# Softmax weights of two batches turned by DMA instead of TensorE, in a fused attention, gated MLP and mixture-of-experts kernel

## The chip, the cores and the metric

The kernel runs on one core of a Trainium2 chip. The metric is the device time of one execution in microseconds (us). One core has TensorE (PE in the profile; weight loads are PEld), VectorE (DVE), ScalarE (ACT), GpSimd (POOL), SyncE (SP, which only issues DMAs here), 16 DMA engines, the on-chip memory SBUF and the matmul result memory PSUM.

## The reference

Three layers in float32, each feeding the next:

```
# attention: 4 batches, 8 heads, 576 positions, head size 64; each query sees at most 32 keys of a band
scores = scale * q @ k.T ; scores = where(mask, scores, -1e9)
attn = exp(scores - max) / (sum + 1e-9) ; x = attn @ v          # x: 2304 tokens x 512
# gated layer
x = ((x @ w_a) * (x @ w_b)) @ w_out                             # 512 -> 1536 -> 512
# routed layer: each token goes to the one of 8 experts with the best cosine score
out[tok] = gate[tok] * (relu(x[tok] @ w1[e]) @ w2[e])
```

## The kernel before

Matrix products keep float32 accuracy by splitting each operand into a high part (`hi`, a rounded copy made by ScalarE) and a low part (`lo`, the remainder, a subtraction on VectorE), and adding three products (`mm3`, lines 768 to 770).

The outer loop runs over batches b = 0 to 3. For each, `f_step(b, f)` is called for f = 0 to 11, one for each 128 columns of the hidden size 1536. A step multiplies the batch's tokens by one slice of w_a and w_b: 24 matmuls of 128x512 for b = 1 and b = 2 (`mm(0, 0)` gives a, `mm(1, 0)` gives b), then `a_copy` (ScalarE, line 813), the product `g` (VectorE, line 819) and, one step later, the high and low parts of g (`g_lows`: ScalarE line 822, POOL line 823). The same step also splits the next step's weight slice, which SyncE has fetched (`ab_load`, line 723): `hi` on ScalarE (line 726), `lo` on VectorE (line 727). After the 12 steps `x1_run` multiplies by w_out.

Woven into the steps of batch b is the attention of batch b + 1, in units of 64 queries, two units to a pair (`AttnPair`; five pairs, the last with one unit). This text says even and odd step for even and odd f; a pair takes an even step, the odd step behind it and the next even one. Before the change, for b = 1 and 2:

- even step: TensorE makes the pair's scores after the first six matmuls of the step (line 584); VectorE adds the mask and takes the maximum for each unit (lines 602, 606); POOL scales the maxima (`least`, line 609); ScalarE takes the exponentials of unit 0 (line 616); VectorE and POOL divide by the sums (`norm`, lines 623 to 625).
- odd step: exponentials and `norm` of unit 1 at its start; in its middle TensorE turns unit 0's weights with four transposes (`trans`, line 633) and ScalarE copies them out of PSUM (line 635).
- next even step: unit 1 is turned at the start, and after six matmuls TensorE makes the products with v (`av`, line 644), directly ahead of the next pair's scores. ScalarE and VectorE then split the result into x0h and x0l (lines 659, 661).

Also in these steps, VectorE computes 32 router dot products ("logits", line 265) for the tokens of the batch before. `Router.steps` takes a list of counts that it cycles through, two entries to a step. SyncE is one queue in program order; in the loop of batch 1 it also issues eight `prefill` writes of 786 KB to memory (line 181). In every engine instructions run in program order, so a waiting one holds all behind it. The program order is written by hand.

Of the kernel before, what the change touches and what calls it, by code (L numbers as in the profile page):

```python
# [87 lines left out]
def fused_kernel(ctx: ExitStack, tc: tile.TileContext, qk, v, wab, wout, w1, w2, emb, tau, cst, msk, out, dbg=None):  # L88
# [380 lines left out]
    class Attn:  # L469
# [3 lines left out]
        def scores(self):  # L473
            b, j = self.b, self.j
            t, jj = qkt[b, j // 3], j % 3
            both = ps.two("odd" if j % 2 else "pair", "sc")[:, :, :192].rearrange("p o (h c) -> p o h c", h=2)
            self.sc = [both[:, odd] for odd in range(2)]
            mt = MASK_OF.get(j, 1)
            m0 = 0 if j == 0 else 1
            if mt == m0:  # L480
                mask = mask_bf[:, mt:mt + 1, :].to_broadcast([128, 2, 96])
            else:
                mask = mask_bf[:, m0:mt + 1:mt - m0, :]
            for sc in self.sc:
                nc.tensor.matmul(out=sc, lhsT=id_bf, rhs=mask, start=True, stop=False)
            for h in range(2):
                for odd in range(2):
                    for p in range(2):
                        pr = 2 * h + odd
                        q = p ^ odd  # L490
                        nc.tensor.matmul(
                            out=self.sc[odd][64 * q:64 * q + 64, h, :],
                            lhsT=t[64 * p:64 * p + 64, pr, 64 * jj:64 * jj + 64],
                            rhs=t[64 * p:64 * p + 64, pr, 192 + 64 * jj:192 + 64 * jj + 96],
                            start=False, stop=h == 1,
                        )
            self.s = at.tile([128, 4, 96], F32, tag="s", name="s", bufs=4)
            mx = at.tile([128, 4], F32, tag="amx", name="amx")
            nc.vector.tensor_reduce(out=mx.rearrange("p (h o) -> p o h", o=2), in_=both, axis=AX.X, op=ALU.max, negate=True)
            self.src = [self.sc[pr % 2][:, pr // 2, :] for pr in range(4)]  # L500
            self.least = at.tile([128, 4], F32, tag="least", name="least")
            nc.gpsimd.tensor_scalar(out=self.least, in0=mx, scalar1=0.125, scalar2=None, op0=ALU.mult)

        def exp(self):
            self.sm = at.tile([128, 4], F32, tag="asm", name="asm")
# [50 lines left out]
    class AttnPair:  # L556
# [33 lines left out]

        def least_of(self):
            n = self.n
            self.s = [at.tile([128, 4, 96], F32, tag="s", name="s", bufs=4) for _ in range(n)]
# [26 lines left out]
        def norm(self, i):  # L620
            if i < self.n:
# [2 lines left out]
                nc.vector.reciprocal(out=sm, in_=sm)  # L624
                nc.gpsimd.tensor_tensor(out=s, in0=s, in1=sm.unsqueeze(2).to_broadcast([128, 4, 96]), op=ALU.mult)

        def trans(self, i):
            if i < self.n:
                if i == 0:
                    self.aT = []  # L630
                tp = ps.tile([96, 4, 128], F32, tag="tp", name="atp")
                for pr in range(4):
                    nc.tensor.transpose(tp[:, pr, :], self.s[i][:, pr, :], ident)
                self.aT.append(at.tile([96, 4, 128], F32, tag="aT", name="aT"))
                nc.scalar.activation(out=self.aT[i], in_=tp, func=AF.Copy)
# [12 lines left out]
                            start=True, stop=True,  # L648
                        )

        def oevac(self):
            hi, lo = x0[self.b]
# [5 lines left out]
            for kk, i, ln, dst in parts:  # L658
                nc.scalar.activation(out=dst(hi), in_=self.o[:, kk, i:i + ln], func=AF.Copy)
            for kk, i, ln, dst in parts:  # L660
                nc.vector.tensor_tensor(out=dst(lo), in0=self.o[:, kk, i:i + ln], in1=dst(hi.bitcast(F32)), op=ALU.subtract)

    def pairs_of(b):
        return [AttnPair(b, list(range(j, min(j + 2, NJ))), b == 1) for j in range(0, NJ, 2)]

    ab_raw, ab_hl = {}, {}
# [124 lines left out]
    def g_lows():  # L791
        while g_low:
            g_low.pop(0)()

    def f_step(b, f, pairs, extra, extra2):
# [6 lines left out]
        prv = pairs[p - 1] if not odd and 0 <= p - 1 < len(pairs) else None  # L802

        def mm(c, hf, ks=range(4)):
            for k in ks:
# [3 lines left out]
        kept = {}  # L809

        def a_copy(hf):
            kept[hf] = ap.tile([128, CH], F32, tag="a", name="a")[:, :CHUNKS[b][hf]]
            nc.scalar.activation(out=kept[hf], in_=acc[0, hf], func=AF.Copy)

        def g_evac(hf):
# [10 lines left out]

        if f - lag in (3, 6, 9):
            load_qk()
        if f - lag in (5, 8, 11):
            load_v()  # L830
        if f < NF - 2:
            ab_load(n + 2)
        if b == 0 and n < 10:
            conv_load(n + 4)
        if n == NF - 1:
# [23 lines left out]
            ab_split(n + 1)  # L859
        else:  # L860
            wo_split(b * NF)
        if len(CHUNKS[b]) == 1:
            mm(0, 0, (0, 1))
            if not odd:
                if prv is not None:
                    prv.av()
                if cur is not None:
                    cur.open()
                    cur.scores()
                    cur.least_of()  # L870
                if prv is not None:
                    prv.oevac()
            g_lows()
            mm(0, 0, (2, 3))
            a_copy(0)
            if cur is not None and not odd:
                cur.exp(0)
            for x in extra:
                x()
            mm(1, 0, (0, 1))  # L880
            if cur is not None and odd:
                cur.trans(0)
            for x in extra2:
                x()
            mm(1, 0, (2, 3))
            if cur is not None and not odd:
                cur.norm(0)
            g_evac(0)
            del ab_hl[n]
            return  # L890
        mm(0, 0)
        a_copy(0)
        if not odd:
# [390 lines left out]
    with tc.manual_schedule():  # L1284
# [61 lines left out]
        for b in range(B):  # L1346
# [5 lines left out]
                pairs = []  # L1352
            steps = iter(())
            if router is not None:
                steps = router.steps((2, 2) if last else (1, 0, 2, 2))
            for f in range(NF):
                extra = []
                extra2 = []
# [25 lines left out]
            if not last:  # L1384
# [13 lines left out]
                if b == B - 2:  # L1398
# [7 lines left out]
                    for q in range(2):  # L1406
                        nc.gpsimd.tensor_copy(out=x0_end[q][:, :, :2 * CARRY], in_=x0_in[b][q][:, :, CH:])
                        nc.gpsimd.tensor_copy(out=x0_end[q][:, :, 2 * CARRY:], in_=x0[b + 1][q][:, :, END0:])
                x1_run(b, hook)
                for _ in steps:  # L1410
                    pass
# [248 lines left out]
```

## Time and profile before

| | |
|---|---|
| time, median of 3 runs | 769.56 us (769.0 to 771.37) |
| time of the profiled execution | 770.28 us |
| its span, first to last instruction | 768.4 us, so 1.9 us lie around it |
| busy TensorE, VectorE, ScalarE, POOL | 98%, 67%, 56%, 30% of the span |
| steps of batch 1, of batch 2 | 79.80 us, 79.64 us (12 steps each) |
| TensorE's granted clock | 1.00 over the span |

The busy share of TensorE says that nearly all of the span has a matmul in it. What a microsecond of another engine's work is worth depends on whether TensorE waits for it in that stretch.

### The profile page before, as it was taken

The page shows a single profiled execution, that of the slowest core. Times are in us where ns is not written, and L with a number is a line of the kernel's source. Part 1 is how long each engine was busy: PE and PEld are TensorE (multiplying, and loading weights), DVE is VectorE, ACT ScalarE, POOL GpSimd, SP SyncE. Part 2 cuts the span into 40 slices and gives each one's busy share as a digit, 9 for nine tenths or more (in the row PEclk, how much of TensorE's full clock was granted, in tenths as well). Part 3 has the DMA queues.
Part 4 walks back from the last instruction along what each step waited for, and adds up shares of the span by engine and source line. Part 5 has one row for each costly group of instructions (what it writes and reads, how often), then busy time and mean ns, then how long its engine had stood idle before and what let it go on. Part 6 is the DMA issues. An engine that isn't in the chain of part 4 may idle for free.

```text
span 768.4 us, 14431 instructions
## 1 busy us (share of the span) xinstructions
PE 755.8 (98%) x5411; PEld 673.4 (88%) x5411; DVE 514.2 (67%) x1067; ACT 429.2 (56%) x950; POOL 229.9 (30%) x261
## 2 busy tenths in 40 slices
PE   8899999999999999999999999999999999999996
PEld 4799998878878888888899999899888999999995
DVE  4788888758887468986267763354666565765672
ACT  5767764356653267662334442375585666767571
POOL 3644444023434224344223524224110001101111
PEclk9999999999999999999999999999999999999999
DMA  9977878577942424222421122835666747757821
GB/s 345 360 235 260 279 278 293 189 276 249 340 159 93 166 65 186 84 83 81 167 71 68 55 83 88 243 110 194 165 226 200 197 135 212 187 169 220 229 90 37
DMA packets 61055, 137.65 MB, mean 179 GB/s; under 512 B 27410, under 2 KB 27666, under 8 KB 58544
## 3 DMA queue, kind: packets, MB, share of 16 engines
q1 hardware_dynamic: 57888, 127.09, 50.7%
q0 software_dynamic: 3088, 9.55, 3.3%
q8 instruction: 44, 0.72, 0.4%
q14 instruction: 35, 0.29, 0.1%
HBM read 106.04 MB, written 25.87 MB: 172 GB/s over the span
## 4 chain that ended last, share of the span: by engine, by line
PE 85%; issue 5%; DMA 4%; DVE 3%; ACT 2%; POOL 1%; POOLq 0%; ACTq 0%; DVEq 0%
PE mm L768 13%; PE mm L770 13%; PE mm L769 12%; PE xr L768 4%; PE xr L769 4%; PE xr L770 4%; DMA out_dram<-yo,ixi 4%; PE hp L770 3%; PE hp L769 3%; PE hp L768 3%; PE xm L770 2%; PE xm L768 2%; PE xm L769 2%; PE ytp L770 2%; PE ytp L768 2%
## 5 line engine op out<-in xcount | busy, mean ns | idle before, releaser
L768 PE MATMUL mm<-x0h,ab 128*128 128x288 f32 (+2 forms) x480 | 171.2, 357 | 0.0
L770 PE MATMUL mm<-x0h,ab 128*128 128x288 f32 (+2 forms) x480 | 166.9, 348 | 0.2 <-DVE ab L727 0.2
L769 PE MATMUL mm<-x0l,ab 128*128 128x288 f32 (+2 forms) x480 | 166.8, 347 | 0.2 <-DVE x0l L553 0.2
L823 POOL TENSOR_TENSOR gl<-g,gh 128x288 fp32r<-128x288 f32 (+2 forms) x60 | 82.7, 1379 | 70.1 <-ACT gh L822 66.7
L768 PEld LDWEIGHTS mm<-x0h,ab 128*128 128x128 f32 x480 | 90.2, 188 | 10.0
L727 DVE TENSOR_TENSOR wl<-raw,wh 128x1024 fp32r<-128x1024 f32 x60 | 73.2, 1224 | 38.2 <-ACT wh L726 37.5
L770 PEld LDWEIGHTS mm<-x0h,ab 128*128 128x128 f32 x480 | 90.1, 188 | 9.6 <-DVE ab L727 0.4
L769 PEld LDWEIGHTS mm<-x0l,ab 128*128 128x128 f32 x480 | 90.2, 188 | 8.5 <-DVE x0l L553 0.5
L1236 POOL DMA_INDIRECT out_dram<-yo,ixi x23 | 25.5, 1107 | 197.3 <-ACT yo L1235 157.1
L726 ACT ACTIVATE wo<-wor 128x512 fp32r<-128x512 f32 x60 | 37.8, 630 | 79.4 <-PE xr L770 50.1
L727 DVE TENSOR_TENSOR wo<-wor,wo 128x512 fp32r<-128x512 f32 x60 | 43.7, 728 | 53.2 <-ACT wo L726 52.6
L727 DVE TENSOR_TENSOR ab<-abr,ab 128x1024 fp32r<-128x1024 f32 x45 | 59.2, 1315 | 26.7 <-ACT ab L726 26.7
L819 DVE TENSOR_TENSOR g<-a,mm 128x288 f32<-128x288 f32 (+2 forms) x72 | 39.5, 549 | 45.8 <-PE mm L770 35.9
L768 PE MATMUL hp<-xTh,wh 128*128 128x352 f32 (+6 forms) x224 | 68.9, 308 | 0.0
L770 PE MATMUL hp<-xTh,wl 128*128 128x352 f32 (+6 forms) x224 | 67.8, 302 | 0.0
L769 PE MATMUL hp<-xTl,wh 128*128 128x352 f32 (+6 forms) x224 | 67.7, 302 | 0.0
L726 ACT ACTIVATE wh<-raw 128x1024 fp32r<-128x1024 f32 x64 | 67.3, 1056 | 0.0
L822 ACT ACTIVATE gh<-g 128x288 fp32r<-128x288 f32 (+2 forms) x60 | 33.1, 551 | 52.1 <-DVE g L819 52.1
L265 DVE SCALAR_TENSOR_TENSOR jl<-rows,en_a 128x512 bf16<-128x512 f32 x60 | 59.0, 983 | 1.2
L726 ACT ACTIVATE ab<-abr 128x1024 fp32r<-128x1024 f32 (+1 forms) x53 | 50.6, 960 | 14.8 <-PE mm L770 8.9
L768 PE MATMUL xr<-wo,gh 128*128 128x512 f32 x144 | 56.4, 392 | 0.0
L770 PE MATMUL xr<-wo,gl 128*128 128x512 f32 x144 | 56.1, 390 | 0.0
(258 smaller groups left out, 1822.2 us busy)
## 6 DMA issues: line engine op xcount, KB each, us to landing
raw<-in_w_dram SPq DMA_DIRECT2D x64, 512.0 KB
abr<-wab SPq DMA_DIRECT2D x36, 512.0 KB
wor<-wout SPq DMA_DIRECT2D x24, 512.0 KB
qkt<-in_qk_dram SPq DMA_DIRECT2D x12, 832.0 KB
vt<-in_v_dram SPq DMA_DIRECT2D x12, 768.0 KB
c<-in_wab_dram SPq DMA_DIRECT2D x8, 1024.0 KB
xs<-rows SPq DMA_DIRECT2D x8, 786.0 KB
wab<-abr SPq DMA_DIRECT2D x12, 512.0 KB
```

The lines of the kernel that those rows point to most:

```text
L265: nc.vector.scalar_tensor_tensor(out=jl, in0=self.rows[:, t, :DM], scalar=1.0, in1=ebox[e // E1][:, e % E1, :], op0=ALU.mult, op1=ALU.mult ...
L726: nc.scalar.activation(out=hi, in_=raw, func=AF.Copy)
L727: (eng or nc.vector).tensor_tensor(out=lo, in0=raw, in1=hi.bitcast(F32), op=ALU.subtract)
L768: nc.tensor.matmul(out=out_, lhsT=lh, rhs=rh, start=first, stop=False)
L769: nc.tensor.matmul(out=out_, lhsT=lh, rhs=rl, start=False, stop=False)
L770: nc.tensor.matmul(out=out_, lhsT=ll, rhs=rh, start=False, stop=last)
L819: nc.vector.tensor_tensor(out=g, in0=kept[hf], in1=acc[1, hf], op=ALU.mult)
L822: nc.scalar.activation(out=hi, in_=g, func=AF.Copy)
L823: nc.gpsimd.tensor_tensor(out=lo, in0=g, in1=hi.bitcast(F32), op=ALU.subtract)
L1236: nc.gpsimd.indirect_dma_start(out=out, out_offset=bass.IndirectOffsetOnAxis(ap=self.ixi[e][:m, t:t + 1], axis=0), in_=yo[:m, :], in_offse ...
```

## The change

For the attention made in the steps of batches 1 and 2 the weights are no longer turned by TensorE:

- `planes` (POOL) copies a unit's weights, as 16-bit halves, into one shared buffer (`turn_box`: 8 blocks of 128 columns, a low and a high half for each of 4 heads); `turn` (SyncE) issues a DMA transpose of that buffer into `pl`, of which there is also one; `join` (ScalarE) puts the halves of 96 rows together again into `aT`.
- `av` moves from the middle of the next even step to the end of the odd step behind it, and the split of its result to the even step after that.
- In even steps VectorE's mask additions and maxima stand ahead of the low part of the next weights. `planes` of unit 1 stands behind the low part of g on POOL.
- Weight slices are loaded up to three steps ahead, so that an even step issues its second load ahead of its `turn`; the loads of v move.
- In batch 1 odd steps hold four logits and even steps one, where it was one and four.
- `s` has 3 buffers for 4, and `a` 1 for 2.

The pieces of the diff that matter here (the new branch ends as the old one did, with `g_evac(0)`):

```diff
+        def planes(self, i):
+            if i < self.n:
+                nc.gpsimd.tensor_copy(
+                    out=turn_box[0].rearrange("p (w h) c -> p w h c", w=2)[:, :, :, :96],
+                    in_=self.s[i].bitcast(U16).rearrange("p h (c w) -> p w h c", w=2))
+
+        def turn(self, i):
+            if i < self.n:
+                self.pl = at.tile([128, 8, 128], U16, tag="pl", name="spl", bufs=1)
+                nc.sync.dma_start_transpose(out=self.pl, in_=turn_box[0].rearrange("p w c -> p (w c)"))
+
+        def join(self, i):
...
+                nc.scalar.activation(
+                    out=self.aT[i].bitcast(U16).rearrange("p h (c w) -> p w h c", w=2),
+                    in_=self.pl[:96].rearrange("p (w h) c -> p w h c", w=2), func=AF.Copy)
...
-            kept[hf] = ap.tile([128, CH], F32, tag="a", name="a")[:, :CHUNKS[b][hf]]
+            kept[hf] = ap.tile([128, CH], F32, tag="a", name="a", bufs=1)[:, :CHUNKS[b][hf]]
...
+        if len(CHUNKS[b]) == 1:
+            old = pairs[p - 2] if not odd and p >= 2 else None
+            if cur is not None and odd:
+                cur.exp(1)
+                cur.norm(1)
...
+            if odd:
+                lows()
+            if old is not None:
+                old.o_high()
+            if prv is not None:
+                prv.join(odd)
+                if not odd:
+                    prv.turn(1)
+            mm(0, 0, (0, 1))
+            if not odd and cur is not None:
+                cur.open()
+                cur.scores()
+                cur.least_of()
+            if not odd:
+                lows()
+            if old is not None:
+                old.o_low()
+            g_lows()
+            if odd and cur is not None:
+                cur.planes(1)
+            mm(0, 0, (2, 3))
+            a_copy(0)
+            if cur is not None and not odd:
+                cur.exp(0)
+            for x in extra:
+                x()
+            mm(1, 0, (0, 1))
+            for x in extra2:
+                x()
+            mm(1, 0, (2, 3))
+            if odd and prv is not None:
+                prv.av()
+            if cur is not None and not odd:
+                cur.norm(0)
+                cur.planes(0)
+                if f + 3 < NF:
+                    ab_load(n + 3)
+                cur.turn(0)
+            g_evac(0)
...
-                steps = router.steps((2, 2) if last else (1, 0, 2, 2))
+                steps = router.steps((2, 2) if last else (2, 2, 1, 0) if b == 1 else (1, 0, 2, 2))
```

On TensorE, at the border of an odd and an even step of batch 1 (`atp` are the turned weights, `av` and `sc` the products with v and the scores, `mm` the step's accumulator), there stood:

```order
L769 MATMUL mm_2257<-x0l,ab 128x512
L770 MATMUL mm_2257<-x0h,ab 128x512
L633 MATMUL atp<-ident,s 96x128 x4
L768 MATMUL mm_2291<-x0h,ab 128x512
L769 MATMUL mm_2291<-x0l,ab 128x512
L770 MATMUL mm_2291<-x0h,ab 128x512
L768 MATMUL mm_2291<-x0h,ab 128x512
L769 MATMUL mm_2291<-x0l,ab 128x512
L770 MATMUL mm_2291<-x0h,ab 128x512
L644 MATMUL av<-aT,vt 64x64 x16
L584 MATMUL sc<-qkt 64x96 x16
```

and now:

```order
L804 MATMUL mm_2405<-x0l,ab 128x512
L805 MATMUL mm_2405<-x0h,ab 128x512
L664 MATMUL av<-aT,vt 64x64 x16
L803 MATMUL mm_2451<-x0h,ab 128x512
L804 MATMUL mm_2451<-x0l,ab 128x512
L805 MATMUL mm_2451<-x0h,ab 128x512
L803 MATMUL mm_2451<-x0h,ab 128x512
L804 MATMUL mm_2451<-x0l,ab 128x512
L805 MATMUL mm_2451<-x0h,ab 128x512
L584 MATMUL sc<-qkt 64x96 x16
```

The transposes are gone, and `av` stands alone at the odd step's end, six matmuls ahead of the scores.

On VectorE, in an even step of batch 2 (`ab` is the low part of the next weights, `s` and `amx` the masked scores and maxima), there stood:

```order
L727 TENSOR_TENSOR ab<-abr,ab 128x1024
L602 TENSOR_TENSOR s<-sc,mask_bf 128x2x2x96
L606 TENSOR_REDUCE amx<-s 128x4
L602 TENSOR_TENSOR s<-sc,mask_bf 128x2x2x96
L606 TENSOR_REDUCE amx<-s 128x4
L661 TENSOR_TENSOR x0l<-av,x0h 128x2x128
```

and now:

```order
L265 SCALAR_TENSOR_TENSOR jl,lg<-rows,en_b 128x512 x2
L854 TENSOR_TENSOR g<-a,mm_3666 128x512
L602 TENSOR_TENSOR s<-sc,mask_bf 128x2x2x96
L606 TENSOR_REDUCE amx<-s 128x4
L602 TENSOR_TENSOR s<-sc,mask_bf 128x2x2x96
L606 TENSOR_REDUCE amx<-s 128x4
L882 TENSOR_TENSOR ab<-abr,ab 128x1024
```

The low part now waits behind the mask additions, and so behind the scores on TensorE.

On SyncE's queue, in the steps of batch 1 (`abr` weight slices, `xs` prefill, `spl` the turned planes), there now stands:

```order
L758 DMA abr<-wab_61 128x1024
L636 DMA_TRANSPOSE spl<-turn 128x8x128
L181 DMA xs<-rows 128x3x524
L758 DMA abr<-wab_61 128x1024
L636 DMA_TRANSPOSE spl<-turn 128x8x128
L181 DMA xs<-rows 128x3x524
L453 DMA qkt<-in_qk_dram 128x1664
```

where the queue held only the `abr`, `xs`, `qkt` and `vt` rows. Two transposes now fall to each pair of steps, each behind a weight slice or a prefill.

## Rows read from the trace of the kernel before

**Rows 1.** Page, busy us of each engine (share of span), instructions:

```profile
PE 755.8 (98%) x5411; PEld 673.4 (88%) x5411; DVE 514.2 (67%) x1067; ACT 429.2 (56%) x950; POOL 229.9 (30%) x261
```

**Rows 2.** Windows: us, busy PE, PEld, DVE, ACT, POOL, clock, DMA share, GB/s:

```profile
157.38:163.90 6.52, 6.52 (x57) 5.13 (x56) 3.27 (x5) 3.31 (x10) 0.24 (x1) 1.00 0.87 344
163.90:205.80 41.90, 41.90 (x361) 34.10 (x360) 34.53 (x67) 27.77 (x84) 17.24 (x17) 1.00 0.85 300
225.45:231.74 6.29, 6.29 (x41) 4.97 (x40) 5.37 (x7) 3.38 (x8) 2.33 (x2) 1.00 0.57 212
231.74:237.18 5.44, 5.44 (x25) 4.50 (x24) 4.32 (x10) 3.36 (x8) 2.87 (x2) 1.00 0.11 44
157.38:237.18 79.80, 79.80 (x613) 64.58 (x612) 65.08 (x124) 49.79 (x138) 31.08 (x29) 1.00 0.69 250
270.13:349.77 79.64, 79.64 (x613) 64.77 (x612) 67.51 (x128) 50.35 (x140) 32.41 (x30) 1.00 0.29 99
296.87:310.82 13.95, 13.95 (x124) 11.40 (x121) 12.80 (x26) 9.04 (x27) 5.24 (x5) 1.00 0.44 153
```

**Rows 3.** Chain of work in batch 2's steps: start, us, what:

```profile
296.68 0.44 PE atp L633 x4
...
298.49 1.08 PE av L644 x32
299.57 0.82 PE sc L584 x32
300.39 0.43 PE mm L768
300.82 0.23 PE mm L769
```

**Rows 4.** Timeline of DVE, batch 2: start, us, engine, line, what:

```profile
299.43 1.22 DVE L727 TENSOR_TENSOR ab<-abr,ab 128x1024 fp32r<-128x1024 f32 x1
300.57 0.55 DVE L602 TENSOR_TENSOR s<-sc,mask_bf 128x384 f32<-128x384 f32 x1
...
302.68 1.00 DVE L661 TENSOR_TENSOR x0l<-av,x0h 128x256 fp32r<-128x256 f32 x3
...
310.39 0.69 DVE L265 SCALAR_TENSOR_TENSOR jl<-rows,en_a 128x512 bf16<-128x512 f32 x1
```

**Rows 5.** Timelines of POOL and of DVE, batch 2, when both are busy:

```profile
303.12 1.30 POOL L823 TENSOR_TENSOR gl<-g,gh 128x512 fp32r<-128x512 f32 x1
...
307.72 2.08 POOL L823 TENSOR_TENSOR gl<-g,gh 128x512 fp32r<-128x512 f32 x1
...
308.59 1.76 DVE L265 SCALAR_TENSOR_TENSOR jl<-rows,en_a 128x512 bf16<-128x512 f32 x1
```

**Rows 6.** The same, a 16-bit copy on POOL beside a logit:

```profile
336.36 1.04 POOL L236 COPY rows<-rows 128x1024 uint16<-128x1024 uint16 x1 [0.53 <-ACT rows L217]
...
336.43 1.52 DVE L265 SCALAR_TENSOR_TENSOR jl<-rows,en_b 128x512 bf16<-128x512 f32 x1
```

**Rows 7.** Timelines of SP and ACT, DMA transposes of 256 and of 128 rows:

```profile
482.72 7.43 SPq L1093 DMA_TRANSPOSE pl<-xs  x1
...
543.96 1.40 SPq L1093 DMA_TRANSPOSE pl<-xs  x1
...
547.25 1.37 ACT L1107 ACTIVATE xf<-pl 128x1024 uint16<-128x1024 uint16 x1 [2.54 <-DMA pl<-xs]
```

**Rows 8.** DMA issues over the span: count, size of one:

```profile
xs<-rows SPq DMA_DIRECT2D x8, 786.0 KB
...
en_a<-en_d SPq DMA_DIRECT2D x1, 1280.0 KB
en_b<-en_d SPq DMA_DIRECT2D x1, 768.0 KB
```

**Rows 9.** Groups of instructions: line, count, busy us, mean ns, idle before:

```profile
L635 ACT ACTIVATE aT<-atp 96x512 f32<-96x512 f32 x27 | 16.1, 595 | 17.2 <-PE atp L633 16.9
```

More of the change, by code (lines that the diff above doesn't have):

```diff
@@ L496, in scores @@
                         )
-            self.s = at.tile([128, 4, 96], F32, tag="s", name="s", bufs=4)
             mx = at.tile([128, 4], F32, tag="amx", name="amx")
@@ L504, in exp @@
         def exp(self):
+            self.s = at.tile([128, 4, 96], F32, tag="s", name="s", bufs=3)
             self.sm = at.tile([128, 4], F32, tag="asm", name="asm")
@@ L592, in least_of @@
             n = self.n
-            self.s = [at.tile([128, 4, 96], F32, tag="s", name="s", bufs=4) for _ in range(n)]
+            self.s = [at.tile([128, 4, 96], F32, tag="s", name="s", bufs=3) for _ in range(n)]
             mx = at.tile([128, 4 * n], F32, tag="amx", name="amx")
@@ L625, in norm @@
                 nc.gpsimd.tensor_tensor(out=s, in0=s, in1=sm.unsqueeze(2).to_broadcast([128, 4, 96]), op=ALU.mult)
+        def planes(self, i):
[8 more added lines that the diff above has]
+        def join(self, i):
+            if i < self.n:
+                if i == 0:
+                    self.aT = []
+                self.aT.append(at.tile([96, 4, 128], F32, tag="aT", name="aT"))
+                nc.scalar.activation(
+                    out=self.aT[i].bitcast(U16).rearrange("p h (c w) -> p w h c", w=2),
+                    in_=self.pl[:96].rearrange("p (w h) c -> p w h c", w=2), func=AF.Copy)
         def trans(self, i):
@@ L649, in av, with parts @@
                         )
-        def oevac(self):
-            hi, lo = x0[self.b]
+        def parts(self):
             j, w = self.js[0], 64 * self.n
@@ L657, in oevac, with o_high, o_low @@
                               lambda t, r=r, m=m, ln=ln: t[:, 2:4, :].rearrange("p k (m r) -> p k r m", r=4)[:, :, r, m:m + ln]))
-            for kk, i, ln, dst in parts:
+            return parts
+        def o_high(self):
+            hi, _ = x0[self.b]
+            for kk, i, ln, dst in self.parts():
                 nc.scalar.activation(out=dst(hi), in_=self.o[:, kk, i:i + ln], func=AF.Copy)
-            for kk, i, ln, dst in parts:
+        def o_low(self):
+            hi, lo = x0[self.b]
+            for kk, i, ln, dst in self.parts():
                 nc.vector.tensor_tensor(out=dst(lo), in0=self.o[:, kk, i:i + ln], in1=dst(hi.bitcast(F32)), op=ALU.subtract)
+        def oevac(self):
+            self.o_high()
+            self.o_low()
+    turn_box = []
     def pairs_of(b):
+        if b == 2:
+            turn_box.append(at.tile([128, 8, 128], U16, tag="tb", name="turn", bufs=1))
+            nc.vector.memset(turn_box[0], 0)
         return [AttnPair(b, list(range(j, min(j + 2, NJ))), b == 1) for j in range(0, NJ, 2)]
@@ L801, in f_step @@
         cur = pairs[p] if 0 <= p < len(pairs) else None
-        prv = pairs[p - 1] if not odd and 0 <= p - 1 < len(pairs) else None
+        prv = pairs[p - 1] if (len(CHUNKS[b]) == 1 or not odd) and 0 <= p - 1 < len(pairs) else None
         def mm(c, hf, ks=range(4)):
@@ L828, in f_step, with lows @@
             load_qk()
-        if f - lag in (5, 8, 11):
+        if f - lag in ((5, 8, 11) if b == 0 else (7, 9)):
             load_v()
-        if f < NF - 2:
+        if f < NF - 2 and n + 2 not in ab_raw:
             ab_load(n + 2)
+        if len(CHUNKS[b]) == 1:
[3 more added lines that the diff above has]
+                cur.norm(1)
+            if f < NF - 1:
+                hi, lo = ab_hl[n + 1] = ab_tile()
+                raw = ab_raw.pop(n + 1)
+                nc.scalar.activation(out=hi, in_=raw, func=AF.Copy)
+            else:
+                wo_split(b * NF)
+            def lows():
+                if f < NF - 1:
+                    nc.vector.tensor_tensor(out=lo, in0=raw, in1=hi.bitcast(F32), op=ALU.subtract)
+            if odd:
[37 more added lines that the diff above has]
+            g_evac(0)
+            if f == NF - 1 and prv is not None:
+                prv.oevac()
+            del ab_hl[n]
+            return
         if b == 0 and n < 10:
@@ L861, in f_step @@
             wo_split(b * NF)
[L862 to L890, printed above, removed]
         mm(0, 0)
@@ L1408, in fused_kernel @@
                         nc.gpsimd.tensor_copy(out=x0_end[q][:, :, 2 * CARRY:], in_=x0[b + 1][q][:, :, END0:])
+                if b == 1:
+                    load_v()
                 x1_run(b, hook)
```

## The prediction

> **What bounds the kernel now.** I began with the busy shares: TensorE is busy 98% of the span [rows 1]. The change touches the steps of batches 1 and 2, so I cut windows there. The 12 steps of batch 1 take 79.80 us and those of batch 2 take 79.64 us, and in both TensorE is busy for the whole window at a granted clock of 1.00, the upper of its two levels, 2.4 GHz [rows 2]. So it waits for nobody, and what comes off its queue comes off the time, until another engine is late.
>
> How near is the next one? In a pair of steps of batch 2, 13.95 us long, VectorE is busy 12.80 us, ScalarE 9.04 and POOL 5.24. In batch 1 VectorE has 34.53 us in three pairs, 11.5 each [rows 2]. VectorE has about 1 us to spare in a pair, and this decides what the change is worth.
>
> **What TensorE saves.** A step without attention (step 11) takes 5.44 us. Step 0 has only the scores of a pair: 6.52, so scores alone cost 1.08. Step 10 has only the products with v of a single unit: 6.29, so those cost 0.85 [rows 2]. In the chain of waits 32 rows of `av` take 1.08 and 32 of `sc` 0.82 [rows 3]; one unit is half of each, 0.54 and 0.41. Entering and leaving such small matmuls thus costs 0.85 - 0.54 = 0.31 for `av` and 1.08 - 0.82 = 0.26 for scores, and today a pair's `av` and the next scores share one entry. Apart, a full pair's `av` costs 1.08 + 0.31 = 1.39, and a single unit's scores 0.41 + 0.26 = 0.67.
>
> The batch after the change: 12 x 5.44 + 4 x 1.08 + 0.67 + 4 x 1.39 + 0.85 = 76.7 us. That is 3.1 less than batch 1's 79.80 and 3.0 less than batch 2's 79.64: **6.1 us**. The transposes alone (nine groups of 0.44 [rows 3] in each batch) would be 7.9; moving `av` away from the scores gives back part of that. A full pair of steps becomes 10.88 + 1.08 + 1.39 = 13.35 us.
>
> **What VectorE must then do in 13.35 us.** It keeps all its instructions. The logits of batch 1 now stand four to an odd step as in batch 2, beside POOL's `norm` and low part of g, so I give both batches batch 2's 12.80. New is POOL's work beside it. A low part of g takes POOL 1.30 us when it meets little and 2.08 against VectorE, and the logit beside it takes 1.76 where one alone takes 0.69 [rows 4, 5]: the two hold each other up. For `planes` the nearest row is a 16-bit copy of 1024 columns, 1.04 us on POOL; the logit beside it took 1.52, 0.83 more than alone [rows 4, 6]. `planes` has 768 columns, three quarters: 0.62 of delay each, 1.24 in a pair if both copies meet such work, nothing if they fall on other work of VectorE. So VectorE needs 12.80 to 14.04 of 13.35: TensorE is held 0 to 0.69 us in a full pair, 0 to 5.5 us over the eight full pairs. I take one copy of the two in full, since `planes` of unit 1 always stands beside the four logits and that of unit 0 at the border to the odd step, and 0.2 of the 1.15 us (13.95 - 12.80) in which VectorE is idle now, because it still waits for ScalarE's high parts and sums: 12.80 + 0.62 + 0.20 - 13.35 = 0.27, **2.2 us** over eight pairs.
>
> The Trainium skill (SBUF — State Buffer, section SBUF: two separate sides) says that VectorE and GpSimd share one pair of ports as an exclusive lock, held for a whole instruction while the other blocks. The trace agrees in kind; in size 0.83 was lost beside a copy of 1.04. By the rule a copy would cost its whole 0.78 instead of 0.62, and the upper bound would be 1.0 a pair, 8.1 in all, which ends 2 us above the time before.
>
> Where lateness is paid: the mask additions now stand ahead of the low part of the next weights. In an even step six matmuls (1.36 us) and the scores (1.08) come first; masks and maxima take 2.11 (300.57 to 302.68) and the low part 1.22 [rows 4], so it is ready 5.8 us into the step, or 7.1 if POOL's low part of g (1.30 [rows 5]) goes first. TensorE wants it after the first two matmuls of the next step, at 6.52 + 0.45 = 7.0. On time it costs nothing; if VectorE reaches the masks more than 1 us late, TensorE waits for the rest.
>
> **ScalarE and POOL.** `join` has the shape of a row of 1.37 us [rows 7] and replaces a copy of 0.60 [rows 9]: 9.04 + 2 x 0.77 = 10.6 of 13.35. POOL gets 2 x 0.78: 6.8 of 13.35. Both fit; hidden under TensorE's matmuls. A waiting `join` holds the high part of g, `a_copy` and the exponentials behind it; TensorE needs that accumulator again only two steps later.
>
> **The DMA chain.** A transpose of 128 rows of the same width was issued at 543.96, held SyncE for 1.40 us and was used at 547.25: 3.29 us [rows 7]. With one buffer on either side, the two transposes of a pair follow each other: turn 0, join 0, turn 1, join 1, then turn 0 of the next pair. That is 2 x (3.29 + 1.37) = 9.3 of 13.35, so free. The far row: 256 rows issued behind other loads held SyncE for 7.43 us [rows 7]; with the 1.89 from there to use, 9.3 us. The chain is late from 13.35 / 2 - 1.37 = 5.3 us on. Batch 2 has a DMA share of 0.29 [rows 2]: I take 3.3 to 4 there. In batch 1 the share is 0.85 in steps 1 to 6 [rows 2], with a prefill of 786 KB in each step [rows 8], and two transposes of up to 1.9 us add 0.2 to 0.3 of a pair. Prefills need not land soon and get out of the way as SyncE issues them later, so I take under 5.3 there too, and keep 9.3 for the range.
>
> The Trainium skill (VectorE: DVE Perf Modes, section The three transpose paths) gives 1309 ns for a DMA turn of one 128x128 block against 390 ns on TensorE, and advises TensorE where a PSUM result will do. Eight blocks in a row would be 10.5 us, an estimate, and the chain 23.7 us a pair, some 80 us slower in all. The row of 3.29 us for all eight blocks speaks against it.
>
> **At nothing.** One buffer of `a`: the next `a_copy` comes 12 matmuls after the last one that g needs, so g has 2.7 us in these steps; if g is late, ScalarE waits there. Three buffers of `s`: a unit's is read out a step or more before it is reused. Moved loads: weight slices are issued earlier than now.
>
> **The sum.** -6.1 + 2.2 = -3.9 us. The profiled execution took 770.28, the median is 769.56, 0.7 lower: 766.4 from the one, 765.7 from the other. I say 766.0.
>
> **The rivals.** A difference under 0.3%, 2.3 us, can't be told from none here: faster is below 767.3, slower above 771.9.
>
> - VectorE takes the place of TensorE. Both copies fall on logits and low parts: 0.69 a pair, and with the 0.2 of idle time 0.89, 5.5 to 7.1 in all: -0.6 to +1.0, 769 to 770.6. For it: 12.80 of 13.35 without any copy. Against it: unit 0's copy partly falls on g and sums. 2.2 in 10. If a copy stops VectorE for all of its 0.78 us, it is 14.36 of 13.35, 8.1 us over eight pairs and 771.6; I give that 1 of the 2.2, since the row shows less. The lock in the Trainium skill (SBUF — State Buffer, SBUF: two separate sides) is this case.
> - Slower: in batch 1 the transposes land late, behind prefills and weight slices in one queue. At 6.5 us each the chain is 15.7 us a pair, 2.4 too long, in the four full pairs 9.6 us: -3.9 + 9.6, 775.3. It decides from 5.3 us; at the far row of 9.3 it would be 8.0 a pair, 32 us. For it: the share of 0.85. Against it: that share holds part of the 2 MB loaded once at batch 1's start (1280 and 768 KB [rows 8]). 2.8 in 10.
> - All is hidden and only TensorE counts: 763.5. 1 in 10.
> - The forecast, 763.5 to 767.3: 4 in 10.
>
> **How the numbers follow.** Faster 0.50 (forecast and all hidden), same 0.22, slower 0.28. The range reaches from just below the all-hidden case, 762.5, to 777, past the late transposes at 6.5 us; longer delays are left out. The likeliest case alone spans 763.5 to 767.3.
>
> **What would show it.** Steps 1 to 8 of batches 1 and 2 at 13.35 to 13.7 us a pair, no atp rows, and no waits of TensorE over 0.5 us: right. Waits of TensorE for the low part (`ab` on VectorE) at odd steps' starts mean VectorE is late; waits of `av` for `aT`, of ScalarE for `spl`, or of POOL's `planes` for the transpose, in batch 1, mean the DMA chain is. Wrong would be a logit that takes no longer beside `planes`, an `av` alone over 1.5 us, or a transpose out of SBUF that takes over 5 us with a free queue.

## The result, and the profile after

The changed kernel takes 774.01 us (median of 8 runs, 773.27 to 777.1) against 770.37 for the kernel before on the same chip: ratio 1.0055, 95% interval 1.0037 to 1.0073. It is slower by some 4 us, on the other side of no change from the 766.0 forecast, and inside the range of 762.5 to 777.0. The profiled span grew from 768.4 to 772.2 us, by 3.8. Both profiled executions had a mean granted clock of 1.00 over the span; in single executions of either kernel it was 0.99, and those took up to 7 us longer than the median.

First the windows of the changed kernel, with the columns of [rows 2]: the steps of batch 1 up to the first row product, the row products behind them (`x1_run`), the steps of batch 2, and one full pair of batch 2.

```profile
157.61:238.72 81.11, 78.01 (x577) 60.73 (x575) 66.42 (x122) 54.07 (x135) 46.41 (x39) 1.00 0.89 257
238.72:273.10 34.38, 33.64 (x154) 26.95 (x150) 18.14 (x42) 11.03 (x20) 9.41 (x15) 1.00 0.49 168
273.10:352.11 79.01, 77.25 (x577) 60.66 (x576) 70.05 (x127) 54.66 (x137) 46.76 (x38) 1.00 0.48 128
299.30:313.39 14.09, 13.59 (x116) 10.49 (x113) 12.93 (x25) 10.38 (x27) 7.76 (x8) 1.00 0.71 173
```

and the row products of batch 1 in the kernel before, which were not shown:

```profile
237.18:270.13 32.95, 32.95 (x151) 27.07 (x149) 16.01 (x38) 10.17 (x18) 9.06 (x16) 1.00 0.41 134
```

TensorE, busy for the whole of these stretches before [rows 2], now has 3.1 us in batch 1 and 1.8 in batch 2 without a matmul. By stage:

| stage | forecast | measured | missed by |
|---|---|---|---|
| steps of batch 1 (79.80 before) | -3.1 + 1.1 | +1.31 | 3.3 |
| row products of batch 1 (32.95) | 0 | +1.43 | 1.4 |
| steps of batch 2 (79.64) | -3.0 + 1.1 | -0.63 | 1.3 |
| row products of batch 2 | 0 | +0.4 | 0.4 |
| routed layer, near 546 us | 0 | +1.4 | 1.4 |

(The last two lines are from the matmuls' start times in the two traces.) Together they miss by 7.8 us, about all of the 7.7 between -3.9 and +3.8.

What TensorE waits for in the steps stands in the waits of batch 1 (two rows) and of batch 2 (one): us in total, times, longest.

```profile
PE mm L805 <- DVE ab L882: 2.0, 3, 0.9
PE av L664 <- ACT aT L643: 1.1, 1, 1.1
```

```profile
PE mm L805 <- DVE ab L882: 1.8, 3, 0.8
```

As the prediction's last part had it, the first kind means that VectorE is late and the second that the DMA chain is. Both occur in batch 1, only the first in batch 2. The list counts less than the stretches lose: it has 1.8 us for batch 2, and the same steps without waits take 76.24 us in a run below, 2.8 less than 79.01. The lengths are the better measure.

How VectorE comes to be late shows when the timelines of one pair of batch 2 are laid beside one another, first VectorE, then POOL, ScalarE and TensorE:

```profile
305.32 0.55 DVE L606 TENSOR_REDUCE amx<-s 128x4 f32<-128x384 f32 x1
305.79 1.22 DVE L882 TENSOR_TENSOR ab<-abr,ab 128x1024 fp32r<-128x1024 f32 x1
...
310.14 0.17 DVE L623 TENSOR_SCALAR asm<-asm 128x4 f32<-128x4 f32 x1 [0.35 <-ACT s L616]
...
311.09 1.84 DVE L882 TENSOR_TENSOR ab<-abr,ab 128x1024 fp32r<-128x1024 f32 x1 [0.57 <-ACT ab L876]
312.85 0.68 DVE L265 SCALAR_TENSOR_TENSOR jl<-rows,en_a 128x512 bf16<-128x512 f32 x1
...
316.00 1.19 DVE L265 SCALAR_TENSOR_TENSOR jl<-rows,en_b 128x512 bf16<-128x512 f32 x1
...
317.12 0.68 DVE L854 TENSOR_TENSOR g<-a,mm 128x512 f32<-128x512 f32 x1
317.72 0.55 DVE L602 TENSOR_TENSOR s<-sc,mask_bf 128x384 f32<-128x384 f32 x1
...
305.96 1.13 POOL L609 TENSOR_SCALAR least<-amx 128x8 f32<-128x8 f32 x1 [3.35 <-DVE amx L606]
...
311.02 0.83 POOL L625 TENSOR_TENSOR s<-s,asm 128x384 f32<-128x384 f32 x1
...
315.74 0.91 POOL L629 COPY turn<-s 128x768 uint16<-128x768 uint16 x1 [1.06 <-DMA spl<-turn]
...
320.00 1.13 POOL L609 TENSOR_SCALAR least<-amx 128x8 f32<-128x8 f32 x1 [3.35 <-DVE amx L606]
...
307.13 0.38 ACT L616 ACTIVATE s<-s,least 128x96 f32<-128x96 f32 x1 [2.21 <-POOL least L609]
...
310.01 1.04 ACT L876 ACTIVATE ab<-abr 128x1024 fp32r<-128x1024 f32 x1
...
307.06 0.50 PE L805 MATMUL mm<-x0h,ab 128*128 128x512 f32 x1 [0.51 <-DVE ab L882]
...
321.10 0.50 PE L805 MATMUL mm<-x0h,ab 128*128 128x512 f32 x1 [0.45 <-DVE ab L882]
```

The reader is to see a ring. POOL scales the maxima at 305.96; ScalarE's eight exponentials wait for that and run from 307.13 to 310.01; the odd step's high part comes behind them in ScalarE's order, the low part (311.09) needs it, four logits, g and the masks stand behind the low part in VectorE's order, and at 320.00 POOL scales the next maxima. From start to start: 1.17 + 2.88 + 1.08 + 1.76 + 4.27 + 0.60 + 2.28 = 14.04 us, the distance of TensorE's two waits. No link of it waits for TensorE: the masks at 317.72 follow g at once, and the scores were there at 315.87. VectorE is busy 12.93 of 14.09 us; of its 1.16 us of idle time 0.92 lie where it waits for ScalarE (0.35 for the last exponentials, 0.57 for the high part), and in this program order nothing stands there that could fill them.

The kernel before had this ring as well (VectorE, then POOL, then TensorE's scores):

```profile
307.16 1.51 DVE L727 TENSOR_TENSOR ab<-abr,ab 128x1024 fp32r<-128x1024 f32 x1 [0.57 <-ACT ab L726]
...
313.08 1.22 DVE L727 TENSOR_TENSOR ab<-abr,ab 128x1024 fp32r<-128x1024 f32 x1
314.41 0.56 DVE L602 TENSOR_TENSOR s<-sc,mask_bf 128x384 f32<-128x384 f32 x1
...
289.29 0.23 POOL L609 TENSOR_SCALAR least<-amx 128x8 f32<-128x8 f32 x1 [6.69 <-DVE amx L606]
...
302.92 0.23 POOL L609 TENSOR_SCALAR least<-amx 128x8 f32<-128x8 f32 x1 [6.76 <-DVE amx L606]
...
316.76 0.23 POOL L609 TENSOR_SCALAR least<-amx 128x8 f32<-128x8 f32 x1 [6.96 <-DVE amx L606]
...
313.45 0.89 PE L584 MATMUL sc<-qkt 64*64 64x96 f32 x32
```

From maxima to maxima it is 13.63 us and then 13.84, beside TensorE's 13.95. The second distance holds a wait for TensorE: the masks start at 314.41, just behind the end of the scores at 314.34, and 1.33 us behind the start of the low part, where it was 1.14 the time before (299.43 to 300.57 [rows 4]). So 13.63 is the ring's own length (in a pair whose scaling takes 0.23 us), and 0.3 us hid it. The change took the even low part (1.14) out of the ring and put into it 0.90 (`least`, which now meets that low part), 0.33 (the odd low part, beside a `norm` that a copy has pushed back) and 0.38 (a logit beside a copy).

POOL's copy from 315.74 to 316.65 and the logit begun at 316.00 show the price of a copy: the logit took 1.19 us for 0.69, 0.50 more, when 0.65 of the copy was left. The Trainium skill (SBUF — State Buffer, section SBUF: two separate sides) has the shared ports held for a whole instruction while the other engine blocks fully; the copy and the logit agree in kind (0.50 of 0.65 us was lost), and the scaling of eight maxima a row in size as well: 0.23 us alone, and 1.13 beside a low part that ends with it.

The DMA issues of the steps near the end of batch 1 (200 to 240 us) and of batch 2 (280 to 345): count, median us from issue to landing. The trace has the landing of three of these four and of six of these nine.

```profile
spl<-turn SPq DMA_TRANSPOSE x4, 5.9
...
spl<-turn SPq DMA_TRANSPOSE x9, 3.3
```

### The profile page after: what moved, and what is told of

Read it like the earlier page. It is cut to its first block, busy times and chain, and to the rows that moved or that the text cites. A ratio compares the mean times of both kernels' runs of the same rounds, so it can differ in the third digit from the quotient of the medians.

```text
span 772.2 us, 14355 instructions
## 1 busy us (share of the span) xinstructions
PE 753.3 (98%) x5339; PEld 665.1 (86%) x5339; DVE 520.2 (67%) x1068; ACT 439.4 (57%) x950; POOL 259.3 (34%) x279
## 5 line engine op out<-in xcount | busy, mean ns | idle before, releaser
L803 PEld LDWEIGHTS mm<-x0h,ab 128*128 128x128 f32 x480 | 90.1, 188 | 10.5
L265 DVE SCALAR_TENSOR_TENSOR jl<-rows,en_a 128x512 bf16<-128x512 f32 x60 | 63.0, 1051 | 1.2
L804 PE MATMUL xr<-wo,gh 128*128 128x512 f32 x144 | 56.5, 393 | 1.1 <-DVE wo L762 1.1
L803 PE MATMUL xr<-wo,gh 128*128 128x512 f32 x144 | 56.8, 394 | 0.0
L805 PE MATMUL ytp<-hTh,wl 128*128 128x336 f32 (+4 forms) x160 | 48.4, 302 | 0.0
```

The source lines that it names most:

```text
L265: nc.vector.scalar_tensor_tensor(out=jl, in0=self.rows[:, t, :DM], scalar=1.0, in1=ebox[e // E1][:, e % E1, :], op0=ALU.mult, op1=ALU.mult ...
L803: nc.tensor.matmul(out=out_, lhsT=lh, rhs=rh, start=first, stop=False)
L804: nc.tensor.matmul(out=out_, lhsT=lh, rhs=rl, start=False, stop=False)
L805: nc.tensor.matmul(out=out_, lhsT=ll, rhs=rh, start=False, stop=last)
```

## The experiments

Every run was timed beside the kernel before, and ratios are to it. All runs but one, which says so, start from the changed kernel (774.0 us, 1.0055).

**The low part's cause: four runs.** First, high and low part of the odd step ahead of the second exponentials:

```diff
             if odd:
                 lows()
+                if cur is not None:
+                    cur.exp(1)
+                    cur.norm(1)
```

(and the high part ahead of it; the two calls are gone from the branch's start).

> In the odd steps the high part of the next weights goes ahead of the second unit's exponentials on ScalarE, and its low part ahead of the second unit's sums on VectorE; nothing else. Theory 'ring': after the change a closed ring sets the pair, not TensorE: masks and maxima 2.1 us (VectorE), least 1.1 (POOL), eight exponentials 2.9 and high part 1.0 (ScalarE), low part 1.2, four logits 4.9 and g 0.7 (VectorE), masks again, 14.0 us of 14.1. Here the low part leaves the ring (it runs while VectorE waits for the exponentials): a pair of batch 2 takes 13.3 to 13.4 us, where TensorE ends it, and the time is 768 to 769.5. Rival 'amount' (VectorE simply has too much work beside POOL's copies): the work is the same, 773 to 775. Rival 'order' (the low part stands behind the masks in even steps, and that alone is late): nothing changes, 773 to 775.

773.08 us, 1.0024 (1.0002 to 1.0045). The total missed. Two of three pairs of batch 2 did as the ring had them; the middle one kept 0.3 us of a wait for the low part:

```profile
288.60:301.93 13.33, 13.33 (x113) 10.38 (x111) 11.99 (x23) 9.62 (x25) 9.14 (x9) 1.00 0.54 118
301.93:315.74 13.81, 13.55 (x117) 10.49 (x113) 13.57 (x25) 10.37 (x27) 8.45 (x7) 1.00 0.77 177
315.74:329.02 13.28, 13.28 (x116) 10.51 (x112) 13.04 (x26) 10.42 (x28) 9.09 (x8) 1.00 0.47 121
```

Batch 1 took it back: in the profiled execution (775.48 us) `av` waits there 4.1 us for `aT` in three places, and behind the third the granted clock falls (last section). With the ring shorter, the DMA chain was late.

Second, the logits:

```diff
-                steps = router.steps((2, 2) if last else (2, 2, 1, 0) if b == 1 else (1, 0, 2, 2))
+                steps = router.steps((2, 2) if last else (1, 1, 2, 1) if b == 1 else (2, 1, 1, 1))
```

> In batches 1 and 2 a pair of steps has three logits in the even step and two in the odd one, not one and four. Ring: two logits leave the ring (0.7 to 1.7 us each) and fall on the 1.1 us in which VectorE waits for the exponentials: a pair of batch 2 at 13.3 to 13.5 us, time 768 to 770. Amount: the same work, 773 to 775. Order: the low part of the odd step's end is reached sooner as well, so no difference to the ring here.

766.5 us, 0.9946 (0.9928 to 0.9964): 7.5 us faster than the changed kernel, and faster than the kernel before; 768 to 770 was expected. Steps of batch 1, its row products, steps of batch 2, a pair of it:

```profile
156.80:235.04 78.24, 76.48 (x578) 61.04 (x576) 66.41 (x121) 54.34 (x135) 46.34 (x39) 1.00 0.91 267
235.04:268.06 33.02, 33.02 (x153) 27.17 (x150) 17.75 (x42) 11.13 (x20) 9.54 (x15) 1.00 0.52 176
268.06:344.30 76.24, 76.24 (x577) 60.95 (x575) 71.72 (x129) 56.17 (x137) 49.31 (x38) 1.00 0.51 133
293.16:306.42 13.26, 13.26 (x117) 10.57 (x113) 13.02 (x25) 10.68 (x27) 8.58 (x8) 1.00 0.80 184
```

VectorE does the same 13.0 us of work in a pair, in 13.26 us instead of 14.09. So the amount of its work was not the bound; where it stood was. One wait stays in batch 1, 1.8 us of `av` for `aT`.

Third, the low part ahead of the masks again:

```diff
+            if not odd:
+                lows()
             if not odd and cur is not None:
                 cur.open()
                 cur.scores()
                 cur.least_of()
-            if not odd:
-                lows()
```

> In the even steps the low part of the next weights goes ahead of the mask additions again, as in the kernel before; nothing else. Order: TensorE's waits for the low part at the odd steps' start (2.6 us in batch 1, 2.2 in batch 2) go away, 768.5 to 770. Ring: the low part's 1.2 us come into the ring, and 0.9 goes out of it, since POOL's scaling of the maxima (1.13 us beside the low part, 0.23 in the kernel before) no longer stands beside it: a pair 14.1 to 14.5 us, 774 to 777. Amount: 773 to 775.

773.47 us, 1.0029 (1.0005 to 1.0053). The waits for the low part are gone and the pairs of batch 2 take 14.38, 14.30 and 14.28 us: `av` now waits for `aT` instead (2.7 us in three places, and 4.1 in four in batch 1). The order of masks and low part alone is not the cause; the ring's forecast of the pair holds, that of the total was a little high.

Fourth, each copy into the planes made twice:

```diff
-            if i < self.n:
+            for _ in range(2 * (i < self.n)):
                 nc.gpsimd.tensor_copy(
```

> POOL makes each copy into the planes twice. Ring with the copies' price in it (small copies gave pairs of 13.6, 13.25 and 13.3 us in batch 2, of 14.24, 14.09 and 14.04): each pair of batch 2 gets 0.4 to 0.8 us longer, 14.5 to 14.9, and in batch 1 the transposes start 0.8 later as well: 777 to 781. Ring without the copies: pairs 14.0 to 14.2, 774 to 775.5.

779.78 us, 1.0125 (1.0083 to 1.0167). Pairs of batch 2: 15.36, 15.10 and 14.62 us, somewhat more than expected. The reverse, copies of 8 columns of 96, which leave the rest of the weights out:

> POOL's copies into the planes take 8 of 96 columns (the rest of the weights is not passed on, so the output is not the attention's); every wait stays. Theory 'ring with the copies' price in it': the logit beside the copy of unit 1 takes 0.69 instead of 1.19 us and one of the sums is 0.6 sooner, so the ring and with it a pair of batch 2 is 0.5 us shorter, 13.6 of 14.1, and the eight pairs give 4 us: 769.5 to 771. Rival 'ring without the copies' (the price lies in the other waits): pair 14.0 to 14.1, 773 to 774.5. The logit beside the small copy shows the price of one copy: 0.62 was taken.

This run's time says nothing about the change: without the attention's weights it took 4667.63 us, and why was not followed up. The steps of batch 2 lie ahead of the routed layer: pairs of 13.58, 13.25 and 13.28 us, the logit beside a copy 0.69. So the copies are in the ring with 0.7 to 0.8 us of a pair, and no less, since at 13.25 TensorE is the bound. VectorE's busy time falls as well here (12.10 us in the pair of 13.25), so it is the run with the logits moved that parts the ring from the amount of work.

**The kernel before with the same order of logits** (the list of the second run, nothing else):

> The kernel before, and in it alone the logits' order of the run with three logits in even steps. Ring: before the change TensorE and the ring both stood at 13.95, so a shorter ring changes nothing: pair of batch 2 13.95, time 769.5 to 771 (same). Rival: the order of the logits is worth its 7 us by itself: 764 to 766.

770.66 us, 1.0013 (0.9991 to 1.0036), a pair 13.94. Where TensorE is the bound, a shorter ring is worth nothing. The distance from maxima to maxima is 13.94 here too, and VectorE's masks wait for TensorE's scores (285 to 330 us: us in total, times, longest):

```profile
DVE s L602 <- PE sc L584: 1.4, 3, 0.5
```

Such a distance is the ring's own length only where none of its links waits for something outside the ring.

**The chain in batch 1.** The prefills on a queue of their own:

```diff
     def prefill(empty, e):
-        nc.sync.dma_start(
+        nc.scalar.dma_start(
```

> The eight prefills of batch 1 are issued by ScalarE instead of SyncE, a queue of their own. Theory 'chain, by the queue': the transposes of batch 1 (5.7 to 5.9 us from issue to landing, 3.3 in batch 2) stand behind prefills in one queue; here they land in 3.3 to 4.5, the waits of the v products for the turned weights (1.5 us) go, pairs of batch 1 take 14.1: 771.5 to 773. Rival 'chain, by the engines': the 16 DMA engines are full whatever the queue, landing stays at 5.5 to 6 or grows, 773.5 to 775.

771.41 us, 1.0019 (0.9995 to 1.0043). The DMA issues from 200 to 240 us:

```profile
xs<-rows ACTq DMA_DIRECT2D x3, 786.0 KB, 7.2
...
spl<-turn SPq DMA_TRANSPOSE x4, 4.0
```

The transposes land in 4.0 us for 5.9 (medians of the three of four whose landing each trace has), no `av` waits, two full pairs of batch 1 take 13.57 and 13.59 us where 14.1 was expected, and its steps 78.27 us, 2.8 less. In this run it was the place in the queue, not the number of bytes: those were about the same. No run takes the prefills out altogether, so what their bytes cost is not measured.

The weight slices of the row products in step 9:

```diff
-                if b and f == NF - 2:
+                if b and f == NF - (3 if b == 1 else 2):
                     wo_load(NPAIR * b)
-                if b and f == NF - 1:
+                if b and f == NF - (3 if b == 1 else 1):
                     wo_load(NPAIR * b + 1)
```

> In batch 1 the first two weight slices of the row products are loaded in step 9, not in steps 10 and 11. Theory 'queue': the row products of batch 1 lose their 1.6 us since those slices are issued at 228.4 and 228.9 (216.4 and 223.4 before), behind SyncE's wait for the last turn, and ScalarE waits 1.5 us for the first: then they take 33 to 33.5 us again, 772 to 773. Rival 'VectorE': it is late with the low parts of wo, since the v products' evacuation and the last logits, slowed by POOL, stand ahead of them: 34.5 to 35.1 us, 773.5 to 774.5.

772.25 us, 1.0031 (1.0011 to 1.0052); the row products of batch 1 take 33.37 us for 34.38. They are issued only 2.3 us sooner, but ahead of two loads of 768 and 832 KB. So the earlier slices alone give back 1.0 of the 1.4 us. But the run with the logits alone has 33.02 with the old loads, though it issues them 9.9 us ahead of the row products, no sooner than the changed kernel (10.3). So the late slices cost something only where VectorE is late as well; the two shares can't be parted.

Both cures together, the logits and the prefills on ScalarE's queue:

> Both: three logits in the even step and two in the odd one, and the prefills issued by ScalarE. Ring and chain together: pairs of both batches at 13.25 us as in the run with the logits alone, and its wait of the v products late in batch 1 (2.0 us) goes: 766.5 less 2 to 2.5, 764 to 765. If ScalarE's issues of the prefills (they hold its exponentials) cost what they save, 766 to 767.

770.33 us, 1.0000 (0.9976 to 1.0024): 4 us worse than the logits alone, a miss. In batch 1 `av` waits 3.1 us in three places, and the clock falls behind the third:

```profile
222.30:225.50 3.20, 1.63 (x34) 1.12 (x33) 0.96 (x4) 1.96 (x3) 0.88 (x2) 1.00 0.38 130
225.50:229.50 4.00, 4.00 (x15) 3.12 (x11) 2.76 (x5) 3.51 (x8) 2.20 (x2) 0.57 0.83 214
```

With pairs of 13.25 us there is less room for the transposes than with 13.6, and prefills on another queue no longer wait when SyncE waits. That this is the reason is argued, not shown. Two transposes of batch 1 whose landing the trace has took 6.7 and 7.5 us here; in the run with the prefills alone none took over 5.5. So an emptier queue does not by itself make the transposes land early.

**DMA in one batch alone**, with the new order of the logits: batch 2's weights by DMA and batch 1's on TensorE at the places of the joins (first), and the reverse (second).

> Three logits in the even step, two in the odd one, and only batch 2's weights turned by DMA; batch 1's on TensorE, where the prefills would have met the transposes. Pairs of batch 1 as on TensorE in the changed order, 14.1, those of batch 2 13.25: 766 to 768. The first transpose of rows late in the program: if any DMA turn earlier makes it land in 4.9 us instead of 3.2, it does so here with 9 of them as well; if it comes from those beside the prefills, it lands in 3.2 here.

> Three logits in the even step, two in the odd one, and only batch 1's weights turned by DMA, batch 2's on TensorE. Pairs of batch 1 13.25 us and the one wait of 2.0, pairs of batch 2 14.1: 768.5 to 770.5. The first transpose of rows late in the program landed in 3.3 us with batch 2's nine turns alone and in 4.7 to 5.0 with all eighteen: if it hangs on those of batch 1, 4.7 to 5.0 here; if on their number, 3.2 to 3.3.

767.03 us, 0.9965 (0.9943 to 0.9986), and 767.87 us, 0.9962 (0.9941 to 0.9983); pairs 14.07 where TensorE turns, 13.25 where the DMA does. In the second `av` waits 0.6 us in step 9 of batch 1, where 2.0 was expected. For the transpose of rows late in the program see below. Both batches on TensorE in the changed order, with the old logits:

```diff
-                prv.join(odd)
-                if not odd:
-                    prv.turn(1)
+                prv.trans(odd)
```

> The changed kernel's order, with the weights turned on TensorE at the places of the joins (no planes, no DMA turn, no join). TensorE gets back 9 x 0.45 in each batch, 14.2 us a pair, and that bounds it, so nothing is gained in the pairs; the waits of the v products (1.5) and the late weights of the row products of batch 1 (1.6) go: 770 to 772. The 1.3 us that the changed kernel loses late, at 546 to 553 us, where a transpose of rows out of DRAM lands in 5.0 us instead of 3.3: if it hangs on the DMA turns earlier in the program, it goes here as well; if it comes with anything else of the change, it stays.

770.75 us, 1.0007 (0.9988 to 1.0026); pairs of 14.08 with TensorE busy throughout. The new order costs 0.13 a pair and nothing in all.

**The version with the lowest time**: the logits, the slices of the row products in step 9, and of the loads of q, k and v in batch 1

```diff
-        if f - lag in (3, 6, 9):
+        if f - lag in ((3,) if b == 1 else (3, 6, 9)):
             load_qk()
-        if f - lag in ((5, 8, 11) if b == 0 else (7, 9)):
+        if f - lag in ((5, 8, 11) if b == 0 else (7,) if b == 1 else (7, 9)):
             load_v()
```

with those left out issued during the row products.

> Three logits in the even step, two in the odd one; in batch 1 two loads of q and k and one of v (2.4 MB) go from steps 6 and 9 into the row products, and the first two weight slices of these into step 9. Theory 'chain, by the queue and by the bytes in it': the one wait of the v products that the logits alone left (2.0 us in step 9, behind a transpose that landed 8.6 us after its issue) goes, and the row products of batch 1 lose nothing: 764 to 765.5. Rival 'by the prefills alone': the loads moved are not what the transposes stand behind, the wait stays, 766 to 767.

765.02 us, 0.9924 (0.9896 to 0.9951): 5 us faster than the kernel before and 9 than the changed one. Its interval overlaps that of the logits alone, so what the moved loads add is not shown. The row products of batch 1 take 33.03 us, and took 33.02 with the logits alone. The wait of `av` in step 9 is shorter than in that run and did not go; the transpose issued at 211.88 still held SyncE for 3.5 us. But the run with DMA in batch 1 alone, whose loads and program order in that batch are those of the logits alone, has the short wait too. In this order, the logits alone, this version, DMA in batch 1 alone:

```profile
PE av L664 <- ACT aT L643: 1.8, 1, 1.8
...
PE av L664 <- ACT aT L643: 0.7, 1, 0.7
...
PE av L664 <- ACT aT L643: 0.6, 1, 0.6
```

So this wait differs by 1.2 us with the loads left where they were, and neither theory is decided.

## Why the prediction was wrong, step by step

**TensorE's saving: right.** 6.1 us, a full pair at 13.35 and a batch at 76.7 were worked out. Without waits a pair takes 13.25 and batch 2 76.24 us, 3.4 less than before.

**VectorE: the step that failed first** is the sentence that took "0.2 of the 1.15 us (13.95 - 12.80) in which VectorE is idle now". All of it stayed: 1.16 us of 14.09, since low part, logits, g and masks stand in a chain behind ScalarE's exponentials and high part. The copies' price of 0.62 was near (0.50 for a logit), and the pair's busy time rose only from 12.80 to 12.93. A sum of busy time against the pair's length was the wrong test. The idle time was one link of a ring over three engines, and the ring's length, 13.63 us, was to be read from the start times of two successive scalings of the maxima, in a pair where no link waits for TensorE. "Where lateness is paid" was right: at the odd steps' start, by the low part. But VectorE reaches the masks 4.3 us into an even step (317.72 in one that starts at 313.39), where six matmuls and the scores, 2.4 us, were counted: three of the four logits and g come first. The price was 14.04 to 14.24 us a pair against 13.25, so 0.8 to 1.0 and not 0.27. Nor are there eight full pairs, over which that was summed: by the prediction's own terms only steps 2 to 7 of a batch hold scores and `av` of full pairs, so there are six in the two batches, and TensorE waits three times in batch 2. The three pairs lose 2.6 of the 2.8 us that batch 2 loses. Of the rivals this is the first, near its upper end, by another mechanism than the amount of work it named: the run with the logits moved leaves the amount as it is and takes the loss away.

**The DMA chain: right in batch 2, wrong in batch 1.** 3.3 to 4 us were taken for a transpose in batch 2: 3.3 in the median, once 5.2. The Trainium skill gives 1309 ns for one 128x128 block (VectorE: DVE Perf Modes, section The three transpose paths). The estimate of 10.5 us for eight, made from it, does not hold: all eight took 3.1 us in a quiet stretch. In batch 1 "I take under 5.3 there too" failed: of six whose landing the trace has, three took 5.9, 6.8 and 8.5 us. Prefills and weight slices stand ahead of a transpose in SyncE's one queue; a transpose held up there holds SyncE, 3.3 us at 215.85, and the next weights behind it came late too: ScalarE waits for them in the last of these rows.

```profile
215.85 3.26 SPq L636 DMA_TRANSPOSE spl<-turn  x1
...
220.80 0.43 SPq L758 DMA_DIRECT2D abr<-wab  x1
...
223.57 1.06 ACT L876 ACTIVATE ab<-abr 128x1024 fp32r<-128x1024 f32 x1 [3.02 <-DMA abr<-wab]
```

So the slower rival had the right place; its size of 9.6 us took every transpose as late, where three of six were, and TensorE's `av` waited once, 1.1 us. Its cost in batch 1 can't be parted cleanly from the ring's: a shorter ring alone brings batch 1 to 78.24 us, an emptier queue alone to 78.27, and both together in that form did worse.

**At nothing: wrong in two places.** "Moved loads: weight slices are issued earlier than now" holds for the steps; the slices of the row products came at 228.4 us for 216.4 and 223.4, behind SyncE's wait for the last turn. Together with VectorE's lateness that cost 1.4 us. And nothing was counted past the steps: 1.4 us went where the routed layer begins (last section); the cause of that stays open.

## What to carry to other kernels

An engine's busy time against a stage's length says whether its work fits, not whether it can be on time: follow one value around the engines to the point where it is needed again, from start times, take out what it waits for an engine outside the ring, and compare that length with the new bound. When the bound falls by 5%, a ring hidden 2% below it can become the bound. Moving work of a busy engine into its own wait (here two logits) was then worth as much as taking most of the new work away (pairs of 13.26 us, and of 13.25 to 13.58 with the small copies). A DMA that the pair waits for is better not issued behind bulk writes in one queue: taking them out of it gave back 2.8 us in batch 1 here, though not together with the shorter ring. A transpose held up there delays the loads behind it.

## What was not expected of the hardware

The first transpose of rows out of memory late in the program, of the same shape and at the same place in the queue, landed later in the changed kernel. Its issue and its first use there, which answer to [rows 7], and in the kernel with both batches on TensorE:

```profile
546.57 1.24 SPq L1158 DMA_TRANSPOSE pl<-xs  x1
...
551.54 1.36 ACT L1172 ACTIVATE xf<-pl 128x1024 uint16<-128x1024 uint16 x1 [4.07 <-DMA pl<-xs]
```

```profile
544.43 1.25 SPq L1152 DMA_TRANSPOSE pl<-xs  x1
...
547.62 1.37 ACT L1166 ACTIVATE xf<-pl 128x1024 uint16<-128x1024 uint16 x1 [2.20 <-DMA pl<-xs]
```

From issue to first use it is 4.97 us against 3.19, and 3.29 before [rows 7]. With the turns of batch 2 alone it was 3.33, with those of batch 1 alone 3.24, and with all eighteen 4.4 to 5.1 in nine kernels. So it follows the number of earlier DMA turns, or something that comes with it; what, stays open.

After waits TensorE's granted clock fell towards the lower level in batch 1: to 0.51 for 3.5 us in the run with the high part first and to 0.57 for 4.0 in the run with both cures, shortly behind stretches in which it had been busy 1.14 of 2.70 and 1.63 of 3.20 us. The first of these:

```profile
226.90:229.60 2.70, 1.14 (x21) 0.65 (x21) 1.32 (x1) 2.41 (x3) 0.82 (x1) 1.00 1.10 386
229.60:230.50 0.90, 0.90 (x18) 0.79 (x19) 0.90 (x2) 0.90 (x3) 0.46 (x1) 1.00 1.00 405
230.50:234.00 3.50, 3.50 (x10) 2.72 (x9) 3.40 (x7) 1.33 (x5) 2.69 (x2) 0.51 0.95 243
```

The run with the low part first had the same, 0.62 for 4.5 us. After the one wait of 1.8 us in the run with the logits alone it did not fall. So in three profiled executions more time went behind a late transpose than its wait. That the waits brought the clock down is not shown: executions of the kernel before had a mean granted clock of 0.99 too, and in its profile TensorE waits nowhere in these steps.
